# Attention and a two-layer product on one core: reciprocal spreads on two queues, a merge put behind the next maximum, and a reordered tail

## The chip, the cores and the metric

The kernel runs on one core of one Trainium2 chip. The metric is device time in microseconds (us). Before the change it is 415.93 us, the median of 4 runs (415.62 to 416.26).

A core has these engines, each with its own queue of instructions that it takes in order: TensorE (PE in the profile; PEld is its weight load), VectorE (DVE), ScalarE (ACT), GpSimd (POOL) and SyncE (SP). SP issues DMAs, POOL and ACT can issue them too. Engines wait for each other by semaphores. TensorE reads SBUF and writes PSUM; POOL has no access to PSUM.

## The reference

For 8 batches and 12 heads with 448 positions of size 64, queries and keys are normalised and attention is computed. Its output, as 3584 rows of 768, goes through a product to 2048 columns, a leaky rectifier, and a product back to 768:

```
q_n, k_n = rmsnorm(q, g_q), rmsnorm(k, g_k)
scores = scale * (q_n @ k_n.T);  scores -= max(scores)
attn = exp(scores);  attn /= sum(attn) + 1e-9
x = (attn @ v) as [3584, 768]
h = x @ w_in;  out = maximum(0.01 * h, h) @ w_out
```

## The kernel before

**Units.** The work of attention is cut into 24 units `u`: a batch and four of its twelve heads. Three units make one batch's input `xts[b]` for the two products. In the steady part, from unit 5 to 22, unit `u` runs in four steps `d` = 0 to 3. Each step issues scores of `u` on PE (L199, one block at d = 0 and two at the others) and their exponents on ACT (L218, `ex`). At d = 0 the unit's maximum is taken on DVE (`shift_max`, L236, then the diagonal `dg`, L238), spread over all partitions by two small matmuls (`shift_mm`, L248) and reduced again on DVE (L249, then `eb`, L257, the bias of all the unit's exponents). Also at d = 0, the values of unit `u - 1` are summed on PE (`pv`, L367) and the denominators too (`zcol`, L307).

**The reciprocals.** ACT takes the logarithm of the denominators (`zcol_ln`, L327) and then the exponent of its negative (`zcol_inv`, L332), which gives `zs`, a column of 128 by 224. Four DMAs spread it into `rz`, 128 by 2 by 448 (L337): `r` picks the half of `rz`, `y` the half of the columns; each moves 112 KB. All four are issued on SP, one after another. SP then issues the loads of unit `u + 4` (L125) and, elsewhere, the DMA transposes of a unit's normalised rows (L183) and the stores (L409). The product of `rz` with the summed values (L347) goes to `xts`. In nine units (8, 9, 12, 14, 15, 18, 20, 21, 22) it is issued on POOL at d = 1, in ten others on DVE. POOL also loads the values of unit `u + 3` (L128) at d = 0, ahead of the reciprocals, and in unit 5 and before it squares the rows of unit `u + 3` (L152).

**The normalisation** of unit `u + 2` is spread over unit `u`: sums of squares (L159) at d = 1, the reciprocal root on ACT (L164, L165) and two products on DVE (L171, `prep_norm`, for queries and keys) at d = 2, then the transpose.

**The two products** are a queue of items that a table, `PLAN`, deals out to the steps (`fill`, L741): after each item one of the step's jobs is issued (load, sum of squares, normalisation and so on). The first product's items (`moe1`, L389) take 18 matmuls for three. The second product, for a pair of 128-row tiles, is done in seven block products instead of eight (`seven`, L471). Its items are `i0` to `i6`, of eight matmuls each (L476), on sums of blocks (`s1` to `s4`, L457 to L466, on DVE; these write `sa`) and of weights (`tw`). What DVE or ACT does with an item's result, here called its merge (`add`, L483, or a copy, L496 and L507), is put into a list `pend` and issued by `flush` at the start of the next item. Each odd batch has two such groups, here A and B, and each even one from batch 2 on has one, here C. By the table, `i6` of a group is the last item of a unit in units 9, 12, 15, 18 and 21. `i4` comes at d = 2 in the same units.

Two rules in the code bear on the change. At the end of d = 3, `flush(keep=True)` issues all that is pending except `s1` to `s4`, which go out behind the next unit's maximum. And `fill` does not issue a job after an item that `merges`, which is `i4`, at d = 2; the job goes out at the end of the step, behind `i4`'s merge.

**The tail.** After unit 23 the last batch's first product runs in a seven-product form as well (`late1`, L602), and its two groups follow with nothing beside them. The first of them is called with `mixed`: its `i0` runs six matmuls of `ma`, four of `mb` (the first half of `sa[:, 1]`), then the last two of `ma`; `i1` runs the other four of `mb`, whose operands the late half of `s2` (L460) writes.

Of the kernel before, what the change touches and what calls it, by code (L numbers as in the profile page):

```python
# [18 lines left out]
def kernel(  # L19
# [11 lines left out]
    nc = tc.nc  # L31
# [25 lines left out]
    def aux(shape, dtype, name):  # L57
        if held:
            return held[0].pop(0)
        return psum.tile(shape, dtype, tag="aux", bufs=4, name=name)  # L60
# [6 lines left out]
    def drop(bank):  # L67
        if held:
            held[0].append(bank)
# [24 lines left out]
    HF = FT // 2  # L94
    HC = DM // 2
    tw = cst.tile([P, 4, HF, HC], FP16)
    sa = cst.tile([P, 4, HF, P], FP16)
# [185 lines left out]
    HS = S // 2  # L283
# [46 lines left out]
    def zcol_inv(u):  # L330
        s = st[u]
        nc.scalar.activation(s["zs"], s["zs"], AF.Exp, bias=0.0, scale=-1.0)  # L332
        s["rz"] = zpool.tile([P, 2, S], FP32, tag="rz", name="rz")
        for r in range(2):
            for y in range(2):
                src = s["zs"][64 * y + r:64 * y + 64:2, None, :]
                nc.sync.dma_start(s["rz"][:, r, HS * y:HS * y + HS], src.broadcast_to([32, 4, HS]))  # L337

    def xmul_sb(u):
        xmul_pool(u, nc.vector)  # L340
# [59 lines left out]
    def col(t):  # L400
        return 64 * (5 - 2 * t) if t < 3 else P * (t - 3)

    def store(pair, t, tile_, c, last):
        for y in range(2):
            n = 2 * t + (1 - y if t < 3 else y)
            b, grp = 2 * pair + n // NS, n % NS
            dst = out[b * S:(b + 1) * S, :].rearrange("(p t) m -> p t m", t=NS)
            eng = nc.scalar if last and y else nc.sync
            eng.dma_start(dst[:, grp, c], tile_[64 * y:64 * y + 64, c])  # L409

    ost = {}
    pend = []
    L, R, LR = slice(0, HC), slice(HC, DM), slice(0, DM)

    def flush(keep=False):
        kept = [p for p in pend if keep and p[0] in (s1, s2, s3, s4)]
        now = [p for p in pend if p not in kept]
        pend[:] = kept
        for fn, args in now:
            fn(*args)  # L420

    def out_tile():
        return opool.tile([P, DM], FP32, tag="ost", name="ost")

    def moe2(pair, t, half, part, late=False):
        flush()
        if half == 0 and part == 0:
            ost[0] = out_tile()
        if part == 0:
            ost[1] = aux([P, 512], FP32, "op2")  # L430
        op2 = ost[1]
        fts = (0, 1, 2, 3, 4, 5, 8, 9, 10, 12, 13, 11, 14, 15, 6, 7) if late else range(FT)
        for i in range(8 * part, 8 * part + 8):
            ft = fts[i]
            nc.tensor.matmul(op2[:, 0:HC], gt[:, ft, ds(col(t), P)], wout16[:, ft, ds(HC * half, HC)],  # L435
                             start=(i == 0), stop=(i == FT - 1))
        if part == 0:
            return
        nc.vector.tensor_copy(ost[0][:, ds(HC * half, HC)], op2[:, 0:HC])
        drop(op2)  # L440
        if half == 1:
            store(pair, t, ost[0], LR, False)

    def wblock(i, j):
        return wout16[:, HF * i:HF * i + HF, HC * j:HC * j + HC]
# [7 lines left out]
    def gblock(t, j):  # L453
        return gt[:, HF * j:HF * j + HF, ds(col(t), P)]
# [13 lines left out]
    def later(fn, *args):  # L468
        pend.append((fn, args))

    def seven(pair, tt, nxt=None, last=False, mixed=False):  # L471
        g = {}

        def mm(bank, a, b, first, fs=range(HF)):
            for f in fs:
                nc.tensor.matmul(bank[:, 0:HC], a[:, f], b[:, f], start=(first and f == 0), stop=(f == HF - 1), skip_group_check=not first)  # L476

        def bank(name):
            g[name] = aux([P, 512], FP32, name)
            return g[name]  # L480

        def add(dst, src, name):
            nc.vector.tensor_tensor(dst, g[name][:, 0:HC], src, op=ALU.add)  # L483

        def put(i, c):
            store(pair, tt[i], g["o"][i], c, last)

        def i0():
            flush()
            g["o"] = (out_tile(), out_tile())  # L490
            ma = bank("ma")
            if mixed:
                mm(ma, gblock(tt[0], 0), wblock(0, 0), True, range(6))
                mm(bank("mb"), sa[:, 1], tw[:, 1], True, range(4))
            mm(ma, gblock(tt[0], 0), wblock(0, 0), True, range(6 if mixed else 0, HF))
            later(lambda: nc.vector.tensor_copy(g["o"][1][:, L], g["ma"][:, 0:HC]))  # L496

        def i1():
            flush()
            mm(g["mb"] if mixed else bank("mb"), sa[:, 1], tw[:, 1], True, range(4 if mixed else 0, HF))  # L500
            later(lambda: add(g["o"][1][:, L], g["o"][1][:, L], "mb"))
            later(lambda: drop(g["mb"]))

        def i2():
            flush()
            mm(g["ma"], gblock(tt[0], 1), wblock(1, 0), False)
            later(lambda: nc.scalar.copy(g["o"][0][:, L], g["ma"][:, 0:HC]))  # L507
            later(lambda: drop(g["ma"]))
            if last:
                later(put, 0, L)  # L510

        def i3():
            flush()
            mm(bank("mc"), sa[:, 0], tw[:, 0], True)
            later(lambda: add(g["o"][1][:, R], g["o"][1][:, L], "mc"))
            if nxt:
                later(s1, nxt)

        def i4():
            flush()  # L520
            mm(bank("md"), sa[:, 2], tw[:, 2], True)
            later(lambda: add(g["o"][1][:, R], g["o"][1][:, R], "md"))
            if last:
                later(put, 1, R)

        i4.merges = True

        def i5():
            flush()
            mm(g["mc"], sa[:, 3], wblock(1, 1), False)  # L530
            if nxt:
                later(s2, nxt)
            later(lambda: add(g["o"][0][:, R], g["o"][1][:, L], "mc"))
            later(lambda: drop(g["mc"]))
            later(put, 0, R if last else LR)
            if nxt:
                later(s3, nxt)
                later(s4, nxt)

        def i6():  # L540
            flush()
            mm(g["md"], gblock(tt[1], 1), tw[:, 3], False)
            later(lambda: add(g["o"][1][:, L], g["o"][1][:, L], "md"))
            later(lambda: drop(g["md"]))
            later(put, 1, L if last else LR)

        return [i0, i1, i2, i3, i4, i5, i6]

    HK = KT // 2
# [191 lines left out]
    def fill(u, d, jobs):  # L741
        for n in range(int(PLAN[u - 3][d])):
            fn = queue.pop(0)[1]
            fn()
            if jobs and not (d == 2 and hasattr(fn, "merges")):
                jobs.pop(0)()
        flush(keep=d == 3 and u < NU - 1)
        for job in jobs:
            job()
# [21 lines left out]
    with tc.manual_schedule():  # L771
# [191 lines left out]
        for u in range(3, NU):  # L963
            for d in range(4):
# [24 lines left out]
                jobs = []  # L989

                def job(fn, *args):
                    jobs.append(lambda: fn(*args))

                if d == 0:
                    if u == 3:
                        prep_norm(4)
                        gate(4)
                    elif narrow(u - 1):
                        if u < NU - 1:
                            job(zcol_inv, u - 1)  # L1000
                    else:
                        xmul(u - 1)
                    if u + 4 < NU:
                        job(load, u + 4)
                    if u + 3 < NU:
                        load_v(u + 3)
                    if u < 6:
                        prep_sqp(u + 3)
                if d == 1 and narrow(u - 1) and not 5 <= u < 8 and ADDED.get(u, 0) < 4:
                    xmul_pool(u - 1)  # L1010
                if u == NU - 1:
                    if d == 1:
                        job(zcol_inv, u - 1)
# [37 lines left out]
                if d == 3 and 6 <= u < NU - 3:  # L1051
                    for ti in range(2):
                        job(prep_sq, u + 3, ALL, (ti,))
                fill(u, d, jobs)
        zsum_slot(NU - 1)
        pv(NU - 1)
        zinv(NU - 1)
        xmul(NU - 1, (0,))
        for i, more in enumerate((((xmul, NU - 1, (1,)), (x_sum, B - 1, 3), (x_sum, B - 1, 1)), ((x_sum, B - 1, 2), (x_sum, B - 1, 4)))):
            c, fn = queue[i]  # L1060
# [33 lines left out]
```

## Time and profile before

| | |
|---|---|
| median of 4 runs | 415.93 us |
| the profiled execution | 415.91 us, of which 414.1 us are the span from the first to the last instruction |
| granted TensorE clock | 0.998 |
| PE busy / idle before L248 in units 13 and 19 | 398.9 us / 0.38 and 1.38 us |
| spread `rz<-zs` on SP | 76 of them, median 0.60 us to issue, 2.3 us from issue to landing |
| load `vt` on POOL's queue | 24 of them, 224 KB, median 5.0 us from issue to landing |
| `xt<-x,rz` (L347) on POOL | 9 of them, median 2.08 us |

A line of the timeline gives the start, the duration, the engine, the line of the kernel, the operation, the output and inputs by name with their shape, the number of instructions merged into the line, and in brackets how long the engine had been idle and who released it. A line with several instructions shows the time they span.

### The profile page before, as it was taken

To read this page: it belongs to the slowest core of one execution; us is meant where nothing else is said; L and a number is where in the kernel's file an instruction comes from. 1 tells how busy PE (TensorE), PEld (TensorE's weight loads), DVE (VectorE), ACT (ScalarE), POOL (GpSimd) and SP (SyncE) were. 2 spreads that over 40 slices of the span, in tenths; PEclk is the share of its full clock that TensorE was granted. 3 is DMA by queue.
4 is the path that set the end of the run, shared out by engine and by line. 5 is a ranking of instruction groups with operands and counts; after the bars stand their busy time and mean duration, and the time that the engine had idled before them with its cause. 6 is when DMAs were issued, how large, how long until landed. Compare 5 with 4: busy or idle time off the path is not lost.

```text
span 414.1 us, 9374 instructions
## 1 busy us (share of the span) xinstructions
PE 398.9 (96%) x3831; PEld 219.7 (53%) x3831; DVE 308.8 (75%) x492; ACT 300.1 (72%) x470; POOL 69.2 (17%) x70
## 2 busy tenths in 40 slices
PE   8689999999999999999999999998999999999995
PEld 7445444554445544554445544454445557558863
DVE  5888798998788666767668756766768788658762
ACT  5998987677886699687887689866986657653600
POOL 1868432200020200020020200003002202000000
PEclk9999999999999999999999999999999999999999
DMA  6999999899665885677664896666562470032023
GB/s 195 281 236 252 242 249 184 202 174 209 135 155 96 222 233 95 154 195 163 161 155 70 217 217 128 171 154 126 193 112 47 120 150 18 9 77 76 2 56 98
DMA packets 71950, 62.41 MB, mean 151 GB/s; under 512 B 36324, under 2 KB 67044, under 8 KB 71908
## 3 DMA queue, kind: packets, MB, share of 16 engines
q1 hardware_dynamic: 61312, 49.62, 47.0%
q0 software_dynamic: 10272, 11.80, 18.3%
q8 instruction: 30, 0.49, 0.5%
q10 hardware_dynamic: 324, 0.39, 0.3%
q14 instruction: 12, 0.10, 0.1%
HBM read 45.61 MB, written 11.01 MB: 137 GB/s over the span
## 4 chain that ended last, share of the span: by engine, by line
PE 82%; DVE 9%; ACT 4%; issue 2%; DMA 1%; SPq 1%; DVEq 0%; ACTq 0%
PE hps L389 27%; PE sT L199 8%; PE op L435 5%; PE sT L367 5%; PE bank L602 5%; PE bank L476 5%; PE ma L476 5%; PE mc L476 4%; PE md L476 4%; DVE n L171 3%; ACT et L218 3%; PE mb L476 2%; PE zc L307 2%; PE warm L769 2%; PE sT L476 1%
## 5 line engine op out<-in xcount | busy, mean ns | idle before, releaser
L218 ACT ACTIVATE et<-sT,eb 128x896 f16<-128x896 f32 x166 | 159.6, 1010 | 23.9 <-PE sT L199 13.9
L389 PE MATMUL hps<-xt,win 128*128 128x448 f16 x600 | 120.8, 353 | 0.2 <-DVE xt L376 0.2
L389 PEld LDWEIGHTS <-win 128*128 128x128 f16 x612 | 56.7, 98 | 58.3 <-issue 9.5
L383 ACT ACTIVATE gt<-hps 128x448 f16<-128x448 f32 x100 | 53.9, 557 | 4.7 <-PE hps L389 4.1
L199 PE MATMUL sT<-qkT 64*64 64x448 f16 x664 | 52.4, 363 | 3.2 <-ACT et L218 2.1
L159 DVE TENSOR_REDUCE ssq<-sq 128x14 f32<-128x896 f32 (+2 forms) x49 | 50.1, 1058 | 0.5 <-ACT sq L148 0.5
L476 PEld LDWEIGHTS <-sa 128*128 128x128 f16 x352 | 32.8, 98 | 26.4 <-issue 5.8
L128 POOL DMA_DIRECT2D vt<-in_v_dram x24 | 17.9, 746 | 168.3 <-PE sT L367 162.2
L322 ACT COPY x<-sT 128x896 f32<-128x896 f32 x16 | 14.5, 907 | 31.4 <-DVE sT L249 31.4
L476 PEld LDWEIGHTS <-gt 128*128 128x128 f16 x264 | 25.3, 98 | 18.4 <-issue 2.1
L199 PEld LDWEIGHTS <-qkT 64*64 64x64 f16 x672 | 15.4, 104 | 36.2 <-issue 31.4
L347 POOL TENSOR_TENSOR xt<-x,rz 128x896 f16<-128x896 f32 x9 | 19.7, 2187 | 82.1 <-DMA rz<-zs 73.8
L236 DVE TENSOR_REDUCE sT<-sT 128x1 f32<-128x896 f32 x22 | 24.1, 1095 | 7.5 <-PE sT L199 7.5
L171 DVE TENSOR_TENSOR n<-rq,rinv 128x896 f16<-128x896 f32 (+2 forms) x25 | 27.0, 1085 | 3.4 <-ACT rinv L165 3.4
L367 PE MATMUL sT<-et,vt 64*64 64x448 f16 x532 | 28.4, 349 | 0.0
L435 PE MATMUL op<-wout,gt 128*128 128x384 f16 x160 | 28.4, 327 | 0.0
L171 DVE TENSOR_TENSOR n<-rk,rinv 128x896 f16<-128x896 f32 (+2 forms) x26 | 28.0, 1084 | 0.0
L292 DVE TENSOR_TENSOR ea<-ea,et 128x896 f16<-128x896 f16 x27 | 16.9, 625 | 13.7 <-ACT et L218 12.3
L367 PEld LDWEIGHTS <-vt 64*64 64x64 f16 x672 | 20.1, 107 | 10.8 <-issue 0.4
L435 PEld LDWEIGHTS <-gt 128*128 128x128 f16 x192 | 17.7, 98 | 13.7 <-issue 3.1
L476 PE MATMUL ma<-wout,gt 128*128 128x384 f16 x128 | 23.5, 326 | 0.0
L148 ACT ACTIVATE sq<-rq 128x896 f32<-128x896 f32 (+2 forms) x18 | 16.3, 913 | 1.3 <-DMA rq<-in_q_dram 1.3
(144 smaller groups left out, 543.4 us busy)
## 6 DMA issues: line engine op xcount, KB each, us to landing
rq<-in_q_dram SPq DMA_DIRECT2D x24, 448.0 KB, 3.8
rk<-in_k_dram SPq DMA_DIRECT2D x24, 448.0 KB, 5.4
out_dram<-ost SPq DMA_DIRECT2D x52, 192.0 KB, 3.2
rz<-zs SPq DMA_DIRECT2D x76, 112.0 KB, 2.3
vt<-in_v_dram POOLq DMA_DIRECT2D x24, 224.0 KB, 5.0
win<-in_moe_w_in_dram POOLq DMA_DIRECT2D x8, 384.0 KB, 15.4
wout<-in_moe_w_out_dram POOLq DMA_DIRECT2D x2, 1536.0 KB, 28.6
out_dram<-ost SPq DMA_DIRECT2D x4, 96.0 KB, 2.1
```

What stands on the lines that cost most here:

```text
L159: nc.vector.tensor_reduce(buf(u, "ssq")[:, ti, :, c[0]:c[1]], buf(u, f"sq{ti}")[:, :, c[0]:c[1]], axis=AXL.X, op=ALU.add)
L171: nc.vector.tensor_tensor(buf(u, "n16")[:, ti, c[0]:c[1]].rearrange("p s a d -> p a s d"), src[:, :, c[0]:c[1]], buf(u, "rinv")[:, ti, :, ...
L199: nc.tensor.matmul(banks[a][64 * r:64 * r + 64, 0:S].rearrange("p (t x) -> p t x", t=NS), kT(u, r, a, t), qT(u, r, a), start=True, stop=True)
L218: nc.scalar.activation(s["et"][:, t], sT[:, :, 0:S], AF.Exp, bias=s["eb"], scale=1.0)
L236: nc.vector.tensor_reduce(s["spare"][:, 511:512], sT[:, :, 0:S], axis=AXL.XY, op=ALU.max)
L347: eng.tensor_tensor(xts[b][:, g], s["x32"], s["rz"], op=ALU.mult)
L367: nc.tensor.matmul(s["pv"][r][64 * a:64 * a + 64, 0:S], vts[u % NV][64 * r:64 * r + 64, a, t], s["et"][64 * r:64 * r + 64, t, a], start=(t ...
L383: nc.scalar.activation(dst, src, AF.Prelu, bias=0.0, scale=1.0, alpha=0.01)
L389: nc.tensor.matmul(hps[:, 0:S], win16[:, kt // 2, kt % 2, ts(ft, P)], xt[:, kt // 2, kt % 2], start=(kt == 0), stop=(kt == KT - 1))
L435: nc.tensor.matmul(op2[:, 0:HC], gt[:, ft, ds(col(t), P)], wout16[:, ft, ds(HC * half, HC)], start=(i == 0), stop=(i == FT - 1))
L476: nc.tensor.matmul(bank[:, 0:HC], a[:, f], b[:, f], start=(first and f == 0), stop=(f == HF - 1), skip_group_check=not first)
L602: nc.tensor.matmul(bank[:, HX * i:HX * i + HX].rearrange("p (t x) -> p t x", t=NS), w, x[:, kt], start=start, stop=(kt == HK - 1), skip_gr ...
```

## The change

Four edits. The spreads with `y` = 1 are issued on POOL's queue instead of SP's. The merge of `i6`, with the release of its bank and its store, becomes one function marked `waits`, and `flush(keep=True)` holds it back too; so in units 9, 12, 15, 18 and 21 it is issued behind the next unit's maximum. The job after `i4` at d = 2 is held back in unit 12 alone; in units 9, 15, 18 and 21 it is now issued behind `i4`'s matmuls and ahead of `i4`'s merge. And in the `mixed` group, `i0` ends with the first four matmuls of the fourth product, `mc`; `i3` does the other four.

```diff
@@ zcol_inv
-                nc.sync.dma_start(s["rz"][:, r, HS * y:HS * y + HS], src.broadcast_to([32, 4, HS]))
+                (nc.sync, nc.gpsimd)[y].dma_start(s["rz"][:, r, HS * y:HS * y + HS], src.broadcast_to([32, 4, HS]))
@@ flush
-        kept = [p for p in pend if keep and p[0] in (s1, s2, s3, s4)]
+        kept = [p for p in pend if keep and (p[0] in (s1, s2, s3, s4) or hasattr(p[0], "waits"))]
@@ seven, i0
             mm(ma, gblock(tt[0], 0), wblock(0, 0), True, range(6 if mixed else 0, HF))
+            if mixed:
+                mm(bank("mc"), sa[:, 0], tw[:, 0], True, range(4))
@@ seven, i3
-            mm(bank("mc"), sa[:, 0], tw[:, 0], True)
+            mm(g["mc"] if mixed else bank("mc"), sa[:, 0], tw[:, 0], True, range(4 if mixed else 0, HF))
@@ seven, i6
-            later(lambda: add(g["o"][1][:, L], g["o"][1][:, L], "md"))
-            later(lambda: drop(g["md"]))
-            later(put, 1, L if last else LR)
+            def end():
+                add(g["o"][1][:, L], g["o"][1][:, L], "md")
+                drop(g["md"])
+                put(1, L if last else LR)
+
+            end.waits = True
+            later(end)
@@ fill
-            if jobs and not (d == 2 and hasattr(fn, "merges")):
+            if jobs and not (d == 2 and u == 12 and hasattr(fn, "merges")):
```

## The prediction

> **What bounds the kernel now.** I read the page's busy shares first, then the waits of TensorE, then the timeline around each wait. Times are in us from the start of the span.
>
> ```profile
> PE 398.9 (96%) x3831; PEld 219.7 (53%) x3831; DVE 308.8 (75%) x492; ACT 300.1 (72%) x470; POOL 69.2 (17%) x70
> ```
>
> PE is the bound. The table by stages of 6 us shows it busy for 6.00 of 6.00 almost everywhere after 60, so an edit can only win what is left of PE's idle time, and anything that makes PE wait is paid in full. The timeline of PE has just two idle stretches worth naming between 60 and 390:
>
> ```profile
> 190.30 0.22 PE L248 MATMUL sT<-dg,onesp 128*128 128x64 f16 x2 [0.38 <-DVE dg L238]
> 286.13 0.22 PE L248 MATMUL sT<-dg,onesp 128*128 128x64 f16 x2 [1.38 <-DVE dg L238]
> ```
>
> Both are PE waiting for the maximum of the unit after a C group (u = 13 and 19). Why DVE is late at 286 is seen in the timelines of DVE and POOL:
>
> ```profile
> 279.16 0.56 DVE L483 TENSOR_TENSOR ost<-md,ost 128x384 f32<-128x384 f32 x1 [0.74 <-PE md L476]
> 279.63 1.08 DVE L171 TENSOR_TENSOR n<-rq,rinv 128x896 f16<-128x896 f32 x1
> 280.63 2.99 DVE L171 TENSOR_TENSOR n<-rk,rinv 128x896 f16<-128x896 f32 x1
> 283.54 0.55 DVE L483 TENSOR_TENSOR ost<-mc,ost 128x384 f32<-128x384 f32 x1
> 284.19 0.56 DVE L483 TENSOR_TENSOR ost<-md,ost 128x384 f32<-128x384 f32 x1
> ...
> 279.63 3.04 POOL L347 TENSOR_TENSOR xt<-x,rz 128x896 f16<-128x896 f32 x1 [9.31 <-DMA rz<-zs]
> ```
>
> The second normalisation takes 2.99 instead of 1.08, and POOL's product 3.04 instead of 2.08. They take turns: POOL waits out the first normalisation, DVE then waits out POOL's 2.08. So a two-operand SBUF instruction of DVE stands still while POOL's L347 runs. The same shows at 120.46 (L463, 1.85 instead of 0.42) and 184.80 (L171, 1.99); DVE was free again 0.13 before POOL's recorded end. DVE instructions that read PSUM beside L347 (L496 at 215.36, 0.56) are not held. This lock decides the case, because the first edit moves the start of L347.
>
> **Part 1, spreads on two queues.** One spread costs SP 0.60 to issue and lands 2.3 after its issue starts (median, 76 of them). In unit 14, zs is ready at 210.38, SP issues at 210.40, 211.0, 211.6 and 212.3, and POOL starts L347 at 214.77, that is 4.39 after zs. Afterwards each queue issues two. No spread on POOL's queue is in the trace, so its landing is bounded. Low: 2.3, as on SP. High: 3.6 to 4.0, the quiet landings of vt on POOL's queue, with four times the bytes read. Between: rq on SP, of vt's read size, lands quietly in 3.5 to 3.7, so the queue itself seems to add 0.1 to 0.5, and I take 2.6, nearest to the same transfer. With 0.05 to wake and 0.7 for the first issue (vt: 0.71 to 0.76; win: 0.63), the last spread lands about 3.4 after zs, so L347 starts about 1.0 earlier (ends: 1.3 earlier, 0.4 later).
>
> The Trainium skill bears on this twice. "DMA: Bandwidth & Descriptors", section "Latency and other measured facts", gives a first byte after about 0.6 us for the hardware path and about 1 us for GpSimd's; by that the landing would be an estimated 2.7 and the start 0.9 earlier. No run here shows it. The same page, "Issuing engines are not separate DMA queues", speaks against the edit: a second issuing engine saves issue time only, which by the 0.60 rows is 1.2 us per unit and no bandwidth.
>
> Is an earlier L347 good? In four units it stands just behind DVE work that PE needs. Unit 14:
>
> ```profile
> 214.03 0.43 DVE L457 TENSOR_TENSOR sa<-gt 128x512 f16<-128x512 f16 x1 [0.33 <-ACT gt L383]
> 214.49 0.43 DVE L460 TENSOR_TENSOR sa<-sa,gt 128x512 f16<-128x512 f16 x1
> 215.36 0.56 DVE L496 COPY ost<-ma 128x384 f32<-128x384 f32 x1 [0.45 <-PE ma L476]
> 215.84 1.30 DVE L463 TENSOR_TENSOR sa<-gt 128x512 f16<-128x512 f16 x1
> ...
> 214.77 2.09 POOL L347 TENSOR_TENSOR xt<-x,rz 128x896 f16<-128x896 f32 x1 [7.27 <-DMA rz<-zs]
> ```
>
> ```profile
> 215.16 1.46 PE L476 MATMUL mb<-tw,sa 128*128 128x384 f16 x8
> ```
>
> L460 writes the second half of the operand of mb, and mb's fifth matmul (about 215.87: 0.65 for the first four) needs it. L347 now comes 0.28 after L460 has begun and only holds L463, which nobody awaits soon. Started 1.0 earlier, at 213.77, it is in before L457 (which ACT holds until 214.03), and DVE is free at 215.7. Then L457 and L460 end at about 216.55 and PE waits 0.7. The same margin stands in unit 20 (L460 310.31, L347 310.59) and unit 8 (119.65, 119.96). Any start from 0.3 to 1.6 earlier costs 0.6 to 1.05 in each; at 0.5 earlier L347 slips in between L457 and L460. In unit 22, L347 (343.12) would come before the second L292 (342.63 to 343.25); it holds that and the L621 copy behind it, which PE's product at 345.06 needs, until 345.6: 0.55. Sum of the losses: 3 x 0.7 + 0.55 = **+2.65**. In units 9, 15 and 21 an L347 that is 1.0 earlier falls beside DVE idle time (1.50 before mc's merge) and costs nothing.
>
> POOL also has 38 more issues, some 25 us on an engine that is 17% busy. Behind them stands L347, which waits for their landing anyway. In unit 5 the squares (L152, 76.15 to 77.83) now stand ahead of two spreads; by 0.7 + 2.6 these land at 81.2, before DVE's L347 at 82.82. By vt's 4.8 they would be 0.5 late: 0 to 0.3 for PE, kept in the range. On SP, loads and stores move up 1.2; no PE wait names them: 0.
>
> **Part 2, the merge of i6 behind the maximum** (after units 9, 12, 15, 18, 21). It takes 0.48 (284.19 to 284.67) from in front of the maximum and puts it between dg and L249, where DVE idles 0.31 (units 13, 19) or 0.70 (10, 16, 22). At most 0.25 falls on eb; ACT's exponent is then late by that, but PE has 3.4 of other products before it needs a slot. So 0 there. The store queues up some 1.5 later on SP; the spreads behind it have 2 in hand.
>
> **Part 3, the job behind i4 is no longer skipped** (units 9, 15, 18, 21; 12 stays). The first normalisation runs in the 0.74 in which DVE waits for md, so DVE gains about 0.7. The md merge comes after it, and i6's products (280.87 in unit 18) need that merge: 278.71 (rinv) + 1.08 + 0.56 = 280.35 is in time, unless L347 holds the normalisation.
>
> In sum for units 18/19: with L347 starting at 277.0 to 278.3 (landings there ran 2.6 to 3.9), normalisations and merges end at about 282.0 to 283.0, PE's scores are there at 282.65, dg at 284.1 to 284.4, and PE arrives at 284.75. The 1.38 goes; I keep back 0.18 for i6 being held: **-1.2**. Units 12/13: L347 ends before L171 starts (0.9 won) and the merge's 0.48 moves: **-0.38**; either alone would do.
>
> **Part 4, four matmuls of mc within i0.** In the tail PE runs dry and waits for the late half of s2:
>
> ```profile
> 393.40 0.44 PEld L476 LDWEIGHTS <-sa 128*128 128x128 f16 x4 [0.54 <-DVE sa L460]
> ```
>
> The six matmuls from 392.12 at 0.1625 end at 393.10; the next starts at 393.40. Four matmuls of mc (0.65), whose operand half has long been written, fill that: **-0.30**, straight into the end. Their bank is the one mc had anyway.
>
> **Sum.** -1.2 - 0.38 - 0.30 + 2.65 = +0.77. The profiled execution took 415.91 (span 414.1 and 1.81 around it), beside a median of 415.93, so no correction: 416.7. About 0.2%, or 0.83 us, is what a measurement of this kernel can tell from no change.
>
> **Rivals.**
> *A, the forecast:* L347 earlier by 0.3 to 1.6, collisions in 8, 14, 20, 22: 416.1 to 417.3. For: the SP landing of 2.3. Against: four separate margins must all be overrun. Chance 0.48.
> *B, faster:* a spread on POOL's queue lands 3.3 to 4.0 after its issue, as vt does. Then L347 stays within +0.3 to -0.4 of its place, no collision arises, and -1.38 - 0.38 - 0.30 = -2.06 remains, or -1.4 at the late end: 413.8 to 414.6. Chance 0.38.
> *C, slower by another road:* POOL's queue lands the spreads over 0.75 later than now (beside loads vt takes 5.8 to 6.3). L347 then holds L463, L466 or L171 for all of its 2.0 in units 8, 14 and 20, where dg has only 0.24 in hand before PE's L248, at about 0.75 each, and costs 0.5 more in unit 12: 2.25 + 0.5 - 1.38 - 0.30 = +1.1, some 417.0, up to 418. Chance 0.10.
> *D, nothing:* the gains and losses are both small, because DVE's slack moves with PE: 415.6 to 416.2. Chance 0.04.
>
> Of A a little under half lies over 0.83 above the time before. Faster by over 0.2%: B, 0.38. Within: 0.26 from A and 0.04 from D, 0.30. Slower: 0.22 from A and 0.10 from C, 0.32. The signs are split, so the range reaches from B to A's upper end, 413.7 to 417.3; A's own is 416.1 to 417.3.
>
> **What would show it.** Right if in the new profile L347 on POOL starts about 3.4 after zs, L460 in units 8, 14 and 20 lasts or starts about 1.7 later, and mb on PE waits on it for 0.7; if the waits of L248 on dg are gone; if PEld no longer waits on L460 in the tail. Wrong if the landing on POOL's queue is 3.3 or more (then B), or if L347 and L460 overlap without holding each other.

## The result and the profile after

The changed kernel takes 417.74 us (median of 37 runs, 415.88 to 419.62) against 416.18 us for the kernel before beside it (56 runs, 415.11 to 417.57). The ratio is 1.0035, with a 95% interval of 1.0027 to 1.0043: slower by about 1.5 us. The sign is the predicted one; the size is twice the forecast, and the time lies above the range's end of 417.3.

The page's busy shares, then the waits of TensorE (who waited for whom, us in total, times, longest):

```profile
PE 399.8 (96%) x3831; PEld 219.5 (53%) x3831; DVE 310.3 (75%) x492; ACT 300.1 (72%) x470; POOL 89.6 (22%) x108
```

```profile
PE mb L476 <- DVE sa L460: 2.4, 3, 0.9
...
PE md L476 <- DVE ost L483: 0.5, 1, 0.5
```

The waits of L248 on dg are gone. In their place stand three waits of `mb` on L460, and one of `md` on a merge. The three are in units 8, 14 and 20. Unit 14, in the timelines of DVE, POOL and PE:

```profile
215.25 0.43 DVE L457 TENSOR_TENSOR sa<-gt 128x512 f16<-128x512 f16 x1 [0.33 <-ACT gt L383]
215.72 2.19 DVE L460 TENSOR_TENSOR sa<-sa,gt 128x512 f16<-128x512 f16 x1
...
211.90 1.09 POOL L337 DMA_DIRECT2D rz<-zs  x2 [3.16 <-ACT zs L332]
215.54 2.08 POOL L347 TENSOR_TENSOR xt<-x,rz 128x896 f16<-128x896 f32 x1 [2.54 <-DMA rz<-zs]
...
217.96 0.82 PE L476 MATMUL mb<-tw,sa 128*128 128x384 f16 x4 [0.76 <-DVE sa L460]
```

L460 takes 2.19 instead of 0.43. L347 was ready while L457 ran, started 0.18 before L460's recorded start, and kept it out until it was done. PE did the first four matmuls of `mb` and then waited.

In unit 18 the first normalisation is held in the same way, and the `md` merge, which now stands behind it, comes too late for `i6`:

```profile
280.02 0.56 DVE L483 TENSOR_TENSOR ost<-mc,ost 128x384 f32<-128x384 f32 x1 [0.67 <-PE mc L476]
280.89 2.25 DVE L171 TENSOR_TENSOR n<-rq,rinv 128x896 f16<-128x896 f32 x1 [0.32 <-ACT rinv L165]
283.07 0.55 DVE L483 TENSOR_TENSOR ost<-md,ost 128x384 f32<-128x384 f32 x1
283.54 1.08 DVE L171 TENSOR_TENSOR n<-rk,rinv 128x896 f16<-128x896 f32 x1
...
280.12 2.08 POOL L347 TENSOR_TENSOR xt<-x,rz 128x896 f16<-128x896 f32 x1 [3.13 <-DMA rz<-zs]
...
283.67 1.46 PE L476 MATMUL md<-tw,gt 128*128 128x384 f16 x8 [0.47 <-DVE ost L483]
```

In the tail, PEld takes all eight weights of `mc` and `mb` without a gap:

```profile
395.02 0.26 PEld L476 LDWEIGHTS <-gt 128*128 128x128 f16 x2
395.35 1.24 PEld L476 LDWEIGHTS <-sa 128*128 128x128 f16 x8
```

**A ledger.** PE's L248 comes once in each unit, so the difference of its start between two profiles, read unit by unit, tells where time came from. Here and below, each column is how much later PE got from one L248 to the next than in the profile before, or, for the tail, from the last L248 to the last eight matmuls.

| profile | up to unit 5 | unit 8 | units 12/13 | unit 14 | units 18/19 | unit 20 | tail |
|---|---|---|---|---|---|---|---|
| changed kernel | +0.73 | +0.93 | -0.46 | +0.93 | -0.81 | +1.06 | -0.32 |

Without the first column this is +1.33. Behind the last matmuls the changed kernel's profile ends another 0.31 later; in the runs below the same end comes from 0.13 sooner to 0.31 later than before, and no run tells why, so it is in no sum here. The first column is no effect of the change: up to there PE's work is the same, and the profiles of the eleven runs below start with anything from -0.29 to +1.26 here.

### The profile page after: what moved, and what is told of

The parts are those of the page before. It is cut to its first block, busy times and chain, and to the rows that moved or that the text cites. A ratio compares the mean times of both kernels' runs of the same rounds, so it can differ in the third digit from the quotient of the medians.

```text
span 416.5 us, 9410 instructions
## 1 busy us (share of the span) xinstructions
PE 399.8 (96%) x3831; PEld 219.5 (53%) x3831; DVE 310.3 (75%) x492; ACT 300.1 (72%) x470; POOL 89.6 (22%) x108
## 4 chain that ended last, share of the span: by engine, by line
PE 77%; DVE 10%; ACT 9%; issue 2%; DMA 1%; SPq 0%; DVEq 0%; ACTq 0%
PE hps L389 23%; PE sT L199 8%; PE op L435 6%; PE sT L367 5%; PE bank L476 5%; PE bank L608 5%; PE md L476 5%; ACT et L218 5%; PE mc L476 5%; PE ma L476 4%; PE zc L307 2%; PE mb L476 2%; DVE n L171 2%; ACT gt L383 2%; DVE sa L460 2%
## 5 line engine op out<-in xcount | busy, mean ns | idle before, releaser
L159 DVE TENSOR_REDUCE ssq<-sq 128x14 f32<-128x896 f32 (+2 forms) x49 | 50.1, 1057 | 1.4 <-ACT sq L148 1.4
L337 POOL DMA_DIRECT2D rz<-zs x38 | 21.1, 559 | 87.8 <-ACT zs L332 49.6
L171 DVE TENSOR_TENSOR n<-rq,rinv 128x896 f16<-128x896 f32 (+2 forms) x25 | 28.2, 1130 | 4.6 <-ACT rinv L165 4.5
L171 DVE TENSOR_TENSOR n<-rk,rinv 128x896 f16<-128x896 f32 (+2 forms) x26 | 26.1, 1010 | 0.0
L347 POOL TENSOR_TENSOR xt<-x,rz 128x896 f16<-128x896 f32 x9 | 19.0, 2116 | 24.1 <-DMA rz<-zs 24.1
```

The source lines that it names most:

```text
L159: nc.vector.tensor_reduce(buf(u, "ssq")[:, ti, :, c[0]:c[1]], buf(u, f"sq{ti}")[:, :, c[0]:c[1]], axis=AXL.X, op=ALU.add)
L171: nc.vector.tensor_tensor(buf(u, "n16")[:, ti, c[0]:c[1]].rearrange("p s a d -> p a s d"), src[:, :, c[0]:c[1]], buf(u, "rinv")[:, ti, :, ...
L337: (nc.sync, nc.gpsimd)[y].dma_start(s["rz"][:, r, HS * y:HS * y + HS], src.broadcast_to([32, 4, HS]))
```

## The experiments

Theory 1, from the prediction: POOL's L347, started earlier, holds L460 in units 8, 14 and 20; the other three edits win. Rival 1: it is the second queue itself, its traffic and its issue, that costs. Rival 2: the moved merge and the unskipped job cost. All ratios are against the kernel before on the same chip.

**All spreads on SP, the other edits kept** (e1_sp_only):

```diff
-                (nc.sync, nc.gpsimd)[y].dma_start(s["rz"][:, r, HS * y:HS * y + HS], src.broadcast_to([32, 4, HS]))
+                nc.sync.dma_start(s["rz"][:, r, HS * y:HS * y + HS], src.broadcast_to([32, 4, HS]))
```

> All four spreads stay on SP, the other three edits as in the changed kernel. Theory 1 (the loss is GpSimd's product L347 starting earlier and holding L460 in units 8, 14 and 20): no wait of mb on L460, no wait of L248 on dg, tail wait gone; 1.4 to 2.1 us faster than before (ratio 0.995 to 0.997). Rival 1 (the loss is the traffic and the issue on a second queue): also faster, by the same. Rival 2 (the moved merge and the unskipped job cost): 0.5 us or more slower than before, with PE waits on dg or on the md merge.

Measured: 413.91 us, ratio 0.9942 (0.9928 to 0.9956). Rival 2 falls: with the three edits alone the kernel is 2.4 us faster, a little more than the 1.4 to 2.1 expected. In the ledger, units 18/19 give -1.44 and the tail -0.33, which is 1.8 of it. One wait on dg stays, 0.35 in unit 13, since L347, behind SP's spreads, made L171 last 2.61 there in this execution instead of 1.08; that is a miss of the expectation.

**The second queue alone, on the kernel before** (e2_queue_only), the reverse of the diff above:

> The kernel before with the spreads on two queues and nothing else. Theory 1: three waits of mb on L460, 2.9 us in all; the waits of L248 on dg at units 13 and 19 shrink by up to 1.7 because L347 is earlier there too: 1.2 to 2.5 us slower than before. Rival 1: slower too, but with the time spread over many places and not in three waits. Rival 2: within 0.5 us of before.

Measured: 417.31 us, ratio 1.0024 (1.0014 to 1.0033). Slower by 1.0, and the ledger names three places: +0.92 in unit 8, +0.94 in unit 20, -0.45 in unit 13, and 0 elsewhere. Two parts of the expectation missed, and with them its size. In unit 14 there was no wait: L347 came just behind L460's start and lost the turn.

```profile
215.07 0.43 DVE L460 TENSOR_TENSOR sa<-sa,gt 128x512 f16<-128x512 f16 x1
...
215.10 2.34 POOL L347 TENSOR_TENSOR xt<-x,rz 128x896 f16<-128x896 f32 x1 [2.75 <-DMA rz<-zs]
```

And the wait of 1.38 in unit 19 stayed, because in unit 18 the spreads landed in up to 5.3 on SP and 5.0 on POOL's queue, so L347 (280.24, in a profile that is 0.59 behind there) was no earlier than before. Where two queues and the loads meet, an earlier start is not sure.

**SP for the three units alone** (e3_sp_in_three):

```diff
-                (nc.sync, nc.gpsimd)[y].dma_start(...)
+                (nc.sync if u in (7, 13, 19) else (nc.sync, nc.gpsimd)[y]).dma_start(...)
```

> The changed kernel, but the spreads that units 8, 14 and 20 use (of units 7, 13 and 19) stay on SP; the other sixteen units use two queues. Theory 1: the three waits of mb on L460 go, 2.9 us, and about 1.5 us faster than before remains (0.995 to 0.998). Rival 1: the traffic is nearly unchanged (32 spreads on GpSimd's queue for 38), so still at least 0.8 us slower than before. Rival 2: as the changed kernel, since edits 2 to 4 stay.

Measured: 414.95 us, ratio 0.9965 (0.9952 to 0.9977). No wait of `mb` on L460; units 8, 14 and 20 give 0 in the ledger, 12/13 -0.45, 18/19 -0.80, tail -0.33. Moving 6 of the 38 spreads back turns the sign.

**All on two queues, but L347 held behind L460** (e4_held):

```diff
-                if d == 1 and narrow(u - 1) and not 5 <= u < 8 and ADDED.get(u, 0) < 4:
+                if d == 1 and narrow(u - 1) and not 5 <= u < 8 and ADDED.get(u, 0) < 4 and u not in (8, 14, 20):
                     xmul_pool(u - 1)
...
                 fill(u, d, jobs)
+                if d == 1 and u in (8, 14, 20):
+                    nc.gpsimd.tensor_copy(gate_t, sa[:, 1, HF - 1, P - 1:P])
+                    xmul_pool(u - 1)
```

> The changed kernel with all spreads on two queues, but in units 8, 14 and 20 GpSimd first copies one column that L460 has written, so L347 starts behind L460; it is issued after the step's items instead of before. Theory 1: L460 lasts 0.43 again, no wait of mb, L463 is held for about 1.5 instead; about 1.5 us faster than before (0.995 to 0.998). Rival 1: same DMAs and same queues, so still at least 0.8 us slower than before.

Measured: 414.26 us, ratio 0.9953 (0.9940 to 0.9965). Unit 14 again:

```profile
213.93 0.42 DVE L460 TENSOR_TENSOR sa<-sa,gt 128x512 f16<-128x512 f16 x1
214.80 0.56 DVE L498 COPY ost<-ma 128x384 f32<-128x384 f32 x1 [0.45 <-PE ma L476]
215.28 1.68 DVE L463 TENSOR_TENSOR sa<-gt 128x512 f16<-128x512 f16 x1
...
214.42 0.19 POOL L1062 COPY gate_t<-sa 128x1 f16<-128x1 f16 x1 [3.22 <-DVE sa L460]
214.60 2.08 POOL L347 TENSOR_TENSOR xt<-x,rz 128x896 f16<-128x896 f32 x1
```

The same DMAs on the same queues, the same lock, now on L463, for which nobody waits; L498 beside it, which reads PSUM, is not held. Rival 1 falls with this run: the queue's traffic is all there and the kernel is 2 us faster than before. The loss is the place of L347.

**The other edits one by one**, each on the kernel before. The matmuls of `mc` (e5_tail):

```diff
+            if mixed:
+                mm(bank("mc"), sa[:, 0], tw[:, 0], True, range(4))
...
-            mm(bank("mc"), sa[:, 0], tw[:, 0], True)
+            mm(g["mc"] if mixed else bank("mc"), sa[:, 0], tw[:, 0], True, range(4 if mixed else 0, HF))
```

> The kernel before with the four early matmuls of mc in the tail alone. Theory 1: the tail's wait of PEld on L460 goes and the last matmuls come 0.3 us earlier (ratio 0.9993, hardly to be told by time; the trace tells). If the matmuls only moved the wait to i3 or i4: 0.

Measured: 415.53 us, ratio 0.9992 (0.9979 to 1.0005), which tells nothing; the trace does: tail -0.32. Its -0.42 in unit 13 is none of the edit's: L347 there stood 0.4 earlier by itself in that execution.

The merge behind the maximum (e6_merge):

```diff
-        kept = [p for p in pend if keep and p[0] in (s1, s2, s3, s4)]
+        kept = [p for p in pend if keep and (p[0] in (s1, s2, s3, s4) or hasattr(p[0], "waits"))]
...
+            end.waits = True
+            later(end)
```

> The kernel before with the merge of i6 behind the maximum alone. Theory 1: dg is 0.48 us earlier, so the 0.38 wait in unit 13 goes and of the 1.38 in unit 19 some 0.9 stay: 0.8 to 0.9 us faster (0.998). Rival 2: slower, by waits for eb.

Measured: 414.94 us, ratio 0.9981 (0.9969 to 0.9993). Unit 13 loses its wait (-0.45), unit 19 keeps 0.64 of 1.38 (-0.73). ACT's waits for eb are those of before (9.7 us in all), so the moved merge delays nothing. In unit 13 this is the edit's only as far as L171, held by L347, lasted about as long as before (1.92 against 1.99); in e5_tail it lasted 1.58, and the wait went without this edit.

The job behind `i4` (e7_job):

```diff
-            if jobs and not (d == 2 and hasattr(fn, "merges")):
+            if jobs and not (d == 2 and u == 12 and hasattr(fn, "merges")):
```

> The kernel before with the job behind i4 no longer held back, unit 12 aside. Theory 1: in unit 18 the first normalisation runs ahead of L347, which then holds the second; the wait in unit 19 falls from 1.38 to about 0.5, unit 13 keeps its 0.38, i6's md products wait for nothing: 0.9 us faster (0.998). Rival 2: the md merge behind the normalisation holds i6's products in units 9, 15, 18 and 21: 0 to 1 us slower.

Measured: 415.22 us, ratio 0.9978 (0.9965 to 0.9991). With SP's later L347 the first normalisation takes its 1.09 and the second is held (2.52), as expected; unit 19's wait is 0.48, a gain of 0.90, and no `md` product waits. Unit 13 did not keep its 0.38, as was expected: it gives -0.35 though nothing was changed there, since L171 lasted 1.63. The line of unit 19:

```profile
285.82 0.22 PE L248 MATMUL sT<-dg,onesp 128*128 128x64 f16 x2 [0.48 <-DVE dg L238]
```

So the 0.47 wait of `md` in the changed kernel belongs to this edit and the second queue together.

**Two queues for unit 11's spreads alone** (e8_one_unit), to win the 0.35 that SP alone had left:

```diff
-                (nc.sync, nc.gpsimd)[y].dma_start(...)
+                (nc.gpsimd if u == 11 and y else nc.sync).dma_start(...)
```

> The three other edits, and two queues for the spreads of unit 11 alone, which unit 12's L347 waits for; all other spreads on SP. Theory 1: in unit 12 L347 starts about 0.5 earlier and holds L171 less, so the 0.35 wait that was left with SP alone goes; the gain in unit 19 (1.4) and in the tail (0.3) stays: 2.2 us faster than before (0.9947) and 0 to 0.4 faster than with SP alone. Rival 1: no different from SP alone.

Measured: 414.08 us, ratio 0.9953 (0.9938 to 0.9968). The ledger has -0.45, -1.43 and -0.32 and no wait of L248 is left, as expected; by time it cannot be told from SP alone. SP alone run again, the last run below, has no such wait either, so it is not shown that this edit removed it.

**A one-operand instruction on POOL** (e9_copy). Units 8, 14 and 20 copy `rz` instead of multiplying:

```diff
-                if d == 1 and narrow(u - 1) and not 5 <= u < 8 and ADDED.get(u, 0) < 4:
+                if d == 1 and narrow(u - 1) and not 5 <= u < 8 and ADDED.get(u, 0) < 4 and u not in (8, 14, 20):
                     xmul_pool(u - 1)
+                if d == 1 and u in (8, 14, 20):
+                    nc.gpsimd.tensor_copy(xts[(u - 1) // NQ][:, (u - 1) % NQ], st[u - 1]["rz"])
```

> The changed kernel, but in units 8, 14 and 20 GpSimd copies rz to its half-precision output instead of multiplying it with the summed values; this leaves that product out for three of the twenty-four units, and GpSimd's instruction has one SBUF operand instead of two. It still waits for all four spreads. If GpSimd's second operand is what makes it hold DVE (theory 1a): L460 lasts 0.43, no wait of mb, about 1.5 us faster than before. If any pass of GpSimd over SBUF holds a two-operand DVE instruction (theory 1b): L460 is held for as long as the copy runs, and mb waits for about that less 1.2.

Measured: 414.82 us, ratio 0.9975 (0.9964 to 0.9985). The copy takes 0.93 to 1.06, and while it runs L460 stands still too in units 8 and 14, and L457 in unit 20 (1.20 for 0.43); it is just too short for `mb` to notice. Unit 14:

```profile
214.53 1.03 DVE L460 TENSOR_TENSOR sa<-sa,gt 128x512 f16<-128x512 f16 x1
...
214.22 1.06 POOL L1018 CAST xt<-rz 128x896 f16<-128x896 f32 x1 [2.42 <-DMA rz<-zs]
```

Theory 1b holds: what holds DVE's two-operand instruction is not POOL's second operand.

**Held, and unit 18's job held back too** (e10_held_skip), beside SP alone once more (e11_sp_again). To e4_held it adds:

```diff
-            if jobs and not (d == 2 and u == 12 and hasattr(fn, "merges")):
+            if jobs and not (d == 2 and u in (12, 18) and hasattr(fn, "merges")):
```

> Two queues for all spreads, L347 held behind L460 in units 8, 14 and 20, and the job behind i4 held back in unit 18 as in unit 12. Theory 1: the 0.47 wait of i6's md products in unit 18 goes as well, so what is left of the change is unit 13 (0.4), unit 19 (1.4) and the tail (0.3): 2.1 us faster than before (0.995), and up to 0.5 faster than with SP alone.

> The kernel with all spreads on SP and the other three edits once more, beside the one above on the same chip. 1.8 to 2.4 us faster than before (0.9942 the first time, within 0.9928 to 0.9956); the one above is faster by 0 to 0.5 if theory 1 has the sizes right.

Measured: 413.97 us, ratio 0.9957 (0.9943 to 0.9971), and 413.73 us, ratio 0.9951 (0.9936 to 0.9965). Both ledgers read -0.45 or -0.46 in unit 13, -1.43 to -1.45 in unit 19 and -0.33 in the tail. The wait of `md` is gone from the first, as expected; the 0 to 0.5 by which it should lead is not there. SP alone also had no wait in unit 13 this time: L347 started 5.2 after zs in unit 12, against 5.8 in e1_sp_only, so that wait comes and goes with the landing. Both beat both kernels; the simplest that does is SP alone.

## Why the prediction was right and wrong

The mechanism was right: who holds whom, three of the four units that were named, and which waits go. The sum of +0.77 was made of terms; the trace puts +1.33 there.

- **Landing, the step that failed.** "I take 2.6" and "about 3.4 after zs": in unit 14 zs was ready at 211.60 and L347 started at 215.54, 3.9 after. POOL began its issues 0.30 after zs, not 0.05 (0.27 after SP); its first issue took 0.55, not 0.7; and its last spread landed in 2.96, not 2.6. POOL's queue adds nothing that shows: in unit 5, where POOL's two spreads run without SP's beside them, they land in 2.2 to 2.3, as SP's did before. What adds is two queues at a time, and that term was missing. Unit 23 shows it with no load beside the spreads; the lines stand below this list. The Trainium skill's "DMA: Bandwidth & Descriptors", section "Latency and other measured facts", has GpSimd's path later by an estimated 0.4; unit 5 does not show that, and the measurement decides.
- **The collisions, mis-sized through it.** L347 was 0.61, 0.45 and 0.32 earlier after zs in units 8, 14 and 20, not 1.0. "At 0.5 earlier L347 slips in between L457 and L460" was priced at up to 1.05 and is what happened; the sum took 0.7 each for the other order. Measured: 0.93, 0.93, 1.06, or 2.92 for 2.10. Of the 0.93 in unit 14, 0.76 is the recorded wait.
- **Unit 22**, 0.55 in the sum, gave 0: 0.3 earlier is too little there.
- **Units 18/19**, -1.2, gave -0.81. The hold of `i6` was seen ("unless L347 holds the normalisation") and priced at 0.18; it took 0.47 as a recorded wait, and 0.63 in the ledger (-0.81 in e4_held against -1.44 in e10_held_skip). L347's start was not the fault here: taken back to the clock of the profile before it is about 278.0, within the stated 277.0 to 278.3.
- **Units 12/13** (-0.38) gave -0.46, though that wait went by itself in e5_tail and e7_job and so may not be the change's; the **tail** (-0.30) -0.32, and the moved merge cost nothing, as said. The spreads late in unit 5 cost nothing either.

The spreads of unit 23 before, of unit 23 after and of POOL's queue in unit 5 after; the last number is the median landing:

```profile
rz<-zs SPq DMA_DIRECT2D x4, 112.0 KB, 2.3
...
rz<-zs SPq DMA_DIRECT2D x2, 112.0 KB, 3.0
rz<-zs POOLq DMA_DIRECT2D x2, 112.0 KB, 2.8
...
rz<-zs POOLq DMA_DIRECT2D x2, 112.0 KB, 2.3
```

Together: +0.82 from the collisions, -0.55 from unit 22, +0.39 from units 18/19 and -0.10 from the last two make the +0.56 between 0.77 and 1.33. That the sum missed by no more is partly luck: the 0.55 that unit 22 did not cost made up for two thirds of the 0.82 that the collisions cost more.

The range failed for a simpler reason. Its upper end was the case's middle plus a little. The text's own bounds, 1.05 three times, made 417.7 with the other terms left as they were (415.91 - 1.88 + 3.15 + 0.55), and that was not carried into it. The kernel before also ran 0.25 above the median that the prediction started from.

Rival B failed narrowly: L347 had to come no more than 0.3 early, and it came 0.32 to 0.61 early. Rival C did not occur: spreads landed in over 5 us once, in unit 18 of e2_queue_only, and even there L347 was no later than before.

**Open:** the changed kernel's times spread over 3.7 us, the four kernels without the collision (e1, e4, e10, e11) over 0.6 to 1.0 in 6 runs each. But the kernel before, which has no collision either, spreads over 2.5 in 56 runs, so 6 runs say little of the spread. That the turn between L460 and L347 is won now by one and now by the other is shown for unit 14 (lost by L347 in e2_queue_only, won in the changed kernel). That this makes most of the spread is only argued: the unchanged first stage alone varies by 1.5, and no run was made to count the turns.

## What to carry to other kernels

Before moving the start of an instruction on GpSimd, look at what VectorE has to do in the next 2 us and who waits for it: earlier was worse here, and a one-column copy that made GpSimd wait for the right VectorE instruction turned 1.5 us of loss into 2 us of gain. When one engine is 96% busy, add up its waits place by place, in the trace: the ledger gave every term of a sum that the time showed only as 0.35%. And when a term has two cases, carry the dearer one into the range.

## What the runs showed of the hardware

A GpSimd pass over SBUF and a VectorE instruction with two SBUF operands exclude each other, whichever has begun, to within 0.15 of GpSimd's recorded end: VectorE stood 1.76 for a 2.08 product (L460, 2.19 for 0.43) and 0.6 for a 1.06 cast, while its PSUM-reading copies beside it ran in 0.54 to 0.56. The unexpected part is the cast, which has one operand. VectorE's own count of operands does matter: its sums of squares (L159), which read one SBUF operand, ran at their usual 1.08 beside L347, as here in unit 15 of the changed kernel:

```profile
232.17 1.08 DVE L159 TENSOR_REDUCE ssq<-sq 128x14 f32<-128x896 f32 x1
...
232.66 2.08 POOL L347 TENSOR_TENSOR xt<-x,rz 128x896 f16<-128x896 f32 x1 [2.38 <-DMA rz<-zs]
```

Splitting four spreads of 112 KB over two queues saved two issues of 0.6 on SP, and each spread's median landing rose from 2.3 to 3.0 on SP and 2.9 on GpSimd's queue; of the 1.2 of issue time that this takes off SP, 0.45 was left for L347 in unit 14. These lines of the DMA issues give the output and input, the queue, the operation, the count, the size and the median landing:

```profile
rz<-zs SPq DMA_DIRECT2D x38, 112.0 KB, 3.0
rz<-zs POOLq DMA_DIRECT2D x38, 112.0 KB, 2.9
```
